# VectorE in place of GpSimd for the token groups' sums and lower halves, one per chunk, and a second buffer for w2's quarters

## The chip, the cores and the metric

The kernel runs on one core of a Trainium2 chip. Its time is the device time of one execution in microseconds (us); before the change the median of 3 runs is 772.16 us (771.65 to 772.54). Engines are named as in the profile: PE is TensorE, DVE is VectorE, ACT is ScalarE, POOL is GpSimd, SP issues the DMAs. Each engine's instructions stand in one order, that of the program.

## What is computed

Attention with sink tokens and a window, then a Fourier mix and a feed-forward layer over 4 x 768 tokens of 512 features:

```python
x = attention(q, k, v, n_sink, window)        # (4, 768, 512)
u = x + real(fft(fft(x, axis=1), axis=2))
un = (u - mean(u)) / sqrt(var(u) + 1e-6)      # over the features
out = u + maximum(un @ w_ch1, 0) @ w_ch2      # 512 -> 2048 -> 512
```

## The kernel before, in words

Attention and the Fourier mix of the four batches come first, up to about 265 us of the profile and at the end beside the first group; none of that is touched. The feed-forward layer then works through 24 blocks of 128 tokens in six groups of four blocks. All of its matmuls run on pairs: a float32 operand is split into an upper half, rounded to the type that PE takes (ACT's cast), and a lower half, which is the operand minus its upper half (a subtraction that reads two tiles in SBUF), and a product takes three matmuls (upper x upper, upper x lower, lower x upper).

**First group (231 to 336 us).** Plain products. Meanwhile the weights arrive, are split, and the seven combinations of w1 that the later groups need are stored to DRAM. At its end `prepare_1` makes the second group's tokens ready.

**Second group (group 1, 337 to 432 us).** The first layer uses seven products in place of eight for a 2 x 2 block matrix (Strassen and Winograd's scheme). `product(n, k, ps)` (L1350) is one of them: 12 matmuls of 256 columns, k = 0 to 6, for each of four chunks `it` of hidden features, into three PSUM banks A, B, C in the order `BANK = "ABCABCB"`; a bank is accumulated on again as soon as DVE or ACT has read it. DVE and ACT add the seven up into four quarters of the hidden layer; `halves` splits a quarter into a slot of `hring` (ACT L1151 upper with the relu, DVE L1152 lower), and `unit` (L1378, 12 matmuls of 512 columns) is the plain second layer of one quarter, one or two quarters behind.

Beside this, `step()` is called ten times for each chunk (40 in all) and plays two tables. `todo` prepares the third group's tokens: `statistics`, `deviate` (14 tiny DVE operations that make 1/sqrt), `make` (L543, the normalized block `un`, one buffer), `turn` (PE transposes it, ACT copies it to `xf`). `w2_at` makes the second layer's weight combinations for the later groups, for eight pairs p of weight tiles: `whole_w2` (DVE L1397, two operations: the whole w2 from its halves, into `sums_r`), `sums_w2` (POOL L1402 to L1405, four operations that read `sums_r`), `split_w2` (ACT L1409 and POOL L1410, twice each), `store_w2` (SP L1415, four DMAs to `td`). `sums_r` has one buffer, so DVE's `whole_w2` of the next pair waits until POOL has read this one. With the last chunk, `sums(2, G)` forms the third group's sums of token quarters (s2, s1, s4 at the chunk's start, s5 later) and their halves x: sums and lower halves on POOL (L1250 to L1261), upper halves on ACT (L1260).

**Last four groups (groups 2 to 5, 432 to 762 us).** Both layers use seven products. The first layer (L1350 again) runs 28 chunks of 12 matmuls; DVE and ACT make from them the quarters X1 to X4 and t, and POOL has its share: X3 = t - X1 and t = X4 + X3 (L1604, L1605) right behind k = 6, and X1 += t (`s1_h`, L1567). The second layer, `product2` (L1517), runs 28 chunks `s2` of 12 matmuls. For chunk s2 + 4, `upper_h` (ACT L1560) and `lower_h` (DVE L1564) split one hidden tile into `hring`, which has four slots: the upper half waits until PE is through with chunk s2. In the same 28 chunks POOL forms X2 -= t at k = 3 (L1635); DVE adds finished PSUM banks to u (`add_u`, L1523: three at once after k = 0), and `sums_x` makes the next group's seven token operands x: sums on POOL (L1542 to L1549), lower halves on DVE or POOL (L1539). Weights stream through eight places of `places`, a load being issued eight products ahead (`load`, L1324).

DVE and POOL both read and write SBUF; the four groups' PSUM reads are DVE's and ACT's.

Of the kernel before, what the change touches and what calls it, by code (L numbers as in the profile page):

```python
# [205 lines left out]
def kernel(  # L206
# [67 lines left out]
    def run(general):  # L274
        tag = "g" if general else ""
        with ExitStack() as p1:
# [942 lines left out]
            def prepare_1():  # L1219
                statistics, deviate, make, turn = prepare(1)  # L1220
                for i in range(4):
                    statistics(i)
                    yield
                for i, _ in enumerate(deviations(*groups[1][0], 4)):
                    if i % 4 == 3:
                        yield
                yield
                for i in range(4):
                    make(i)
                    yield  # L1230
                    turn(i, banks[1][0], "n")
                    yield
                start, put = sums(1, V)
                start()
                for k in range(7):
                    yield
                    put(k)

            def sums(n, eng):

                xf = state["xf"]
                a11, a12, a21, a22 = (xf[:, i, 2 * j:2 * j + 2] for i in range(2) for j in range(2))
                sm = state.setdefault("s", {})

                def new(k):
                    sm[k] = npool.tile([P, 2, 256], F32, tag="qs0", name=f"s{k}_{n}", bufs=QSB)
                    return sm[k]

                def start():
                    eng.tensor_tensor(new(2), a21, a22, op=ALU.add)  # L1250
                    eng.tensor_tensor(new(1), sm[2], a11, op=ALU.subtract)
                    eng.tensor_tensor(new(4), a11, a21, op=ALU.subtract)

                def put(k):
                    if k == 5:
                        eng.tensor_tensor(new(5), a12, sm[1], op=ALU.subtract)
                    x = {0: a11, 3: a12, 6: a22}.get(k)
                    x = sm[k] if x is None else x
                    hi, lo = (t[:, k].rearrange("p (c t) -> p c t", c=2) for t in state["x"])
                    A.copy(hi, x)  # L1260
                    eng.tensor_tensor(lo, x, f32(hi), op=ALU.subtract)  # L1261

                return start, put

# [68 lines left out]
            with tc.manual_schedule():  # L1333
# [60 lines left out]
                def whole_w2(p):  # L1394
                    for j in range(2):
                        w = Wt[2 * p + j, 1]
                        V.tensor_tensor(sums_r[:, j], f32(w[0]), f32(w[1]), op=ALU.add)  # L1397

                def sums_w2(p):
                    q = [sums_t[p % 2][i // 2][1][:, i % 2] for i in range(4)]  # L1400
                    b11, b12, b21, b22 = (sums_r[:, i, 256 * j:256 * j + 256] for i in range(2) for j in range(2))
                    G.tensor_tensor(q[1], b12, b11, op=ALU.subtract)  # L1402
                    G.tensor_tensor(q[0], b22, q[1], op=ALU.subtract)
                    G.tensor_tensor(q[2], b12, b22, op=ALU.subtract)
# [22 lines left out]
                for n in range(LDB, NWS):  # L1427
                    load(n)
                n = 0
                statistics, deviate, make, turn = prepare(2)  # L1430
                todo = {0: [(statistics, 0)], 1: [(statistics, 1, 2)], 2: [(statistics, 3)], 3: [(deviate,)], 4: [(make, 0)], 6: [(turn, 0, *banks[1][:2]), (make, 1)],
                        8: [(turn, 1, *banks[1][:2]), (make, 2)], 11: [(turn, 2, *banks[0][:2]), (make, 3)], 13: [(turn, 3, *banks[0][:2])]}
                turn_ = 0
                for it in range(NIT):
                    put = lambda k: None
                    if it == NIT - 1:
                        start, put = sums(2, G)
                        start()

                    def step():  # L1440
# [7 lines left out]
                    for k in range(7):  # L1448
# [33 lines left out]
                        step()  # L1482
                while done[0] < len(units):
                    unit(1)
                assert not w2_at, w2_at
# [17 lines left out]
                def get(i, b, name):  # L1503
                    pool, t = sets[i]["ABC".index(b)]
                    return pool.tile([P, 512], F32, tag=t, name=name, bufs=1)

                def product2(s2, k, c, n, ps):
                    h = hring[:, s2 % 4]
# [21 lines left out]
                def sums_x(g):  # L1530

                    xf = state["xf"]
                    a11, a12, a21, a22 = (xf[:, i, 2 * j:2 * j + 2] for i in range(2) for j in range(2))
                    s2 = npool.tile([P, 2, 256], F32, tag="un", name=f"sx_{g}", bufs=1)

                    def put(k, x, eng):
                        hi, lo = (t[:, k].rearrange("p (c t) -> p c t", c=2) for t in state["x"])
                        A.copy(hi, x)
                        eng.tensor_tensor(lo, x, f32(hi), op=ALU.subtract)  # L1539

                    return {
                        6: lambda: G.tensor_tensor(a21, a11, a21, op=ALU.subtract),  # L1542
                        7: lambda: G.tensor_tensor(s2, a22, a21, op=ALU.subtract),
                        8: lambda: put(0, a11, V),
                        9: lambda: put(3, a12, G),
                        10: lambda: put(1, s2, V),
                        11: lambda: G.tensor_tensor(a11, a11, s2, op=ALU.add),
                        14: lambda: put(4, a21, V),
                        16: lambda: G.tensor_tensor(a12, a12, s2, op=ALU.subtract),  # L1549
                        17: lambda: put(2, a11, G),  # L1550
                        19: lambda: put(5, a12, G),
                        21: lambda: put(6, a22, V),
                    }

                def upper_h(n):

# [7 lines left out]
                    V.tensor_tensor(*args, op=ALU.subtract)  # L1564

                def s1_h(c):
                    G.tensor_tensor(X[1][c], X[1][c], t_[c], op=ALU.add)  # L1567

                for g in range(2, len(groups)):
                    more_ = g + 1 < len(groups)  # L1570
                    todo = {}
# [6 lines left out]
                    for it in range(0, NIT, 2):  # L1578
                        for k in range(7):
                            for i in range(2):  # L1580
# [32 lines left out]
                                if t in (16, 17):  # L1613
                                    s1_h(t - 16)
                                for fn, *args in todo.pop(t - (7 if g > 2 else 0), ()):
                                    fn(*args)
                                t += 1
                    assert not todo
# [2 lines left out]
                    for s2 in range(7 * NIT):  # L1621
# [9 lines left out]
                            lower_h(s2 + 4, upper_h(s2 + 4))  # L1631
                        if s2 < 2:
                            s1_h(2 + s2)
                        if k == 3:
                            G.tensor_tensor(X[2][c], X[2][c], t_[c], op=ALU.subtract)  # L1635
                        if c == NIT - 1:
                            for half, m in (((0, 1), (1, 0), (1, 1)), ((0, 1),), ((1, 1),), ((0, 0),), ((1, 1),), ((0, 1),), ((1, 0),))[k]:
                                add_u(g, half, m, p)
                            if k >= 5:
                                store_u(g, k - 5)  # L1640
                        if g == 2 and 6 <= s2 < 6 + NPR:
                            f = s2 - 6
                            for a in range(2):
                                nc.sync.dma_start(f32(Wt[2 * f, 1][a])[:, 256:], t_dram[f][:, 3, 256 * a:256 * a + 256])
                        if s2 in xs:
                            xs[s2]()

    run(False)
    general = nc.values_load(outside[0:1, 0:1])
# [79 lines left out]
```

## Time and profile before

| what | before |
|---|---|
| median of 3 runs | 772.16 us |
| the profiled execution | 770.74 us |
| its span in the profile | 769.0 us |
| PE busy | 725.7 us (94%) |
| DVE busy | 555.6 us (72%) |
| POOL busy | 410.6 us (53%) |
| ACT busy | 350.0 us (46%) |
| chain that ended last | PE 63%, DVE 20%, POOL 7% |

The profiled execution took 1.74 us more than its span and 1.42 us less than the median. In the profile a line such as `493.64 1.77 DVE L1564 TENSOR_TENSOR hring<-x,hring` reads: start, duration, engine, line of the kernel, operation, the tile written and the tiles read, then shape and type and how many instructions were merged; in brackets the idle time of the engine ahead of it and who ended it. PEclk is the clock that PE was granted, as a share of the full one.

### The profile page before, as it was taken

Reading aid. Unit: us, or ns where it says so; the run is one execution under the profiler, and the core shown is the slowest. Engines: PE = TensorE matmul, PEld = TensorE weight load, DVE = VectorE, ACT = ScalarE, POOL = GpSimd, SP = SyncE. Lnnn points to the kernel's source line nnn. Section 1 sums busy time; section 2 is a strip of 40 time slices with the busy share of each in tenths; the row PEclk is TensorE's granted clock in tenths of the full one; section 3 lists DMA queues with packets and bytes.
Section 4 is the critical chain, followed back from the end, with each engine's and each line's share of the span. In section 5 each row is a group of like instructions: output and inputs, shape, how many; then the busy total and the mean of one; then the engine's idle time right before and its main releaser. Section 6 shows DMA issues by size and latency. Waiting matters only on the chain.

```text
span 769.0 us, 15770 instructions
## 1 busy us (share of the span) xinstructions
PE 725.7 (94%) x5539; PEld 646.3 (84%) x5539; DVE 555.6 (72%) x1251; ACT 350.0 (46%) x887; POOL 410.6 (53%) x487
## 2 busy tenths in 40 slices
PE   7999999989989889899989999999999999999996
PEld 5676876867878767678779999899998999899996
DVE  6877577887899988876763745957599467943683
ACT  4787666667533235413323244433454144523441
POOL 2567477476557878725978134810485046603430
PEclk9999999999999999999999999999999999999998
DMA  9863535432218798799988698959974897659731
GB/s 305 259 168 113 155 85 171 141 115 97 97 55 284 249 340 300 255 326 380 300 290 250 236 354 287 314 195 393 346 268 128 299 390 248 227 191 394 280 108 60
DMA packets 109577, 181.70 MB, mean 236 GB/s; under 512 B 9868, under 2 KB 44812, under 8 KB 108336
## 3 DMA queue, kind: packets, MB, share of 16 engines
q1 hardware_dynamic: 109200, 176.83, 67.7%
q0 software_dynamic: 288, 3.76, 1.2%
q8 instruction: 46, 0.75, 0.4%
q14 instruction: 43, 0.35, 0.1%
HBM read 148.04 MB, written 32.51 MB: 235 GB/s over the span
## 4 chain that ended last, share of the span: by engine, by line
PE 63%; DVE 20%; POOL 7%; issue 5%; ACT 3%; DMA 2%; SPq 0%; DVEq 0%; ACTq 0%; POOLq 0%
PE qB L1517 9%; PE pB L1350 9%; PE pA L1350 6%; PE qC L1517 6%; PE pC L1350 6%; PE qA L1517 4%; PE xt L839 4%; PE s L744 4%; PE o L1378 3%; PE pt L801 2%; PE za L398 2%; PE h L661 2%; DVE sm L763 1%; PE o L1159 1%; DVE hring L1564 1%
## 5 line engine op out<-in xcount | busy, mean ns | idle before, releaser
L1604 POOL TENSOR_TENSOR x<-u,x 128x512 f32<-128x512 f32 x16 | 22.8, 1427 | 163.0 <-ACT u L1603 163.0
L1564 DVE TENSOR_TENSOR hring<-x,hring 128x512 fp32r<-128x512 f32 x92 | 88.9, 993 | 6.2 <-ACT hring L1560 5.7
L1560 ACT CAST hring<-x 128x512 fp32r<-128x512 f32 x92 | 56.9, 618 | 54.9 <-PE qB L1517 15.8
L769 ACT ACTIVATE sm<-sm,mx 128x132 f32<-128x132 f32 x192 | 76.0, 400 | 4.9 <-DVE mx L763 4.9
L1350 PE MATMUL pB<-x,w_b 128*128 128x256 f32 x528 | 68.2, 283 | 0.0
L1350 PEld LDWEIGHTS pB<-x,w_b 128*128 128x128 f32 x528 | 64.9, 191 | 0.1
L661 PE MATMUL h<-un_slots,w_ring 128*128 128x512 f32 x192 | 50.4, 411 | 7.1 <-DVE h L1152 6.9
L744 PE MATMUL s<-ring,q 64*128 64x260 f32 x320 | 49.2, 411 | 7.5 <-DVE mx L763 3.7
L763 DVE CUSTOM_DVE_ANT_0 sm<-s,mask 128x132 f32<-128x132 f32 x192 | 48.5, 293 | 7.5 <-PE s L742 1.9
L661 PEld LDWEIGHTS h<-un_slots,w_ring 128*128 128x128 f32 x192 | 36.6, 197 | 17.1 <-DVE h L1152 6.7
L1350 PE MATMUL pC<-x,w_b 128*128 128x256 f32 x336 | 42.5, 281 | 2.6 <-DVE tmp L1471 2.6
L744 PEld LDWEIGHTS s<-ring,q 64*128 64x128 f32 x320 | 26.9, 185 | 20.1 <-issue 5.0
L1517 PE MATMUL qA<-w,hring 128*128 128x256 f32 x312 | 40.7, 281 | 3.1 <-DVE hring L1564 3.1
L1350 PEld LDWEIGHTS pC<-x,w_b 128*128 128x128 f32 x336 | 40.7, 189 | 3.4 <-DVE tmp L1471 3.3
L780 POOL CAST sk<-sm 128x32 fp32r<-128x32 f32 x48 | 11.1, 232 | 58.2 <-ACT sm L769 58.1
L1517 PEld LDWEIGHTS qA<-w,hring 128*128 128x128 f32 x312 | 38.2, 189 | 3.7 <-DVE hring L1564 3.7
L1159 PE MATMUL o<-w,h 128*128 128x512 f32 x156 | 39.1, 395 | 1.0 <-POOL w L629 0.4
L808 ACT COPY pta<-pt 128x512 f32<-128x512 f32 x48 | 28.1, 585 | 26.0 <-PE pt L801 25.9
L1378 PE MATMUL o<-w,hring 128*128 128x512 f32 x156 | 38.4, 393 | 1.4 <-DVE hring L1152 1.4
L839 PE MATMUL xt<-ptl,ldv 128*64 128x128 f32 x384 | 39.3, 285 | 0.0
L1517 PE MATMUL qB<-w_c,hring 128*128 128x256 f32 x288 | 37.6, 284 | 0.2
L817 POOL TENSOR_SCALAR_AFFINE_SELECT ptl<-pta 128x512 f32<-128x512 f32 x48 | 31.3, 652 | 11.6 <-ACT pta L808 11.6
(289 smaller groups left out, 1996.1 us busy)
## 6 DMA issues: line engine op xcount, KB each, us to landing
w_b<-wd SPq DMA_DIRECT2D x184, 256.0 KB, 4.8
w_c<-wd SPq DMA_DIRECT2D x96, 256.0 KB, 5.0
raw<-in_moe_w_ch_dram SPq DMA_DIRECT2D x32, 512.0 KB, 4.9
w_c<-td SPq DMA_DIRECT2D x48, 256.0 KB, 4.4
w_b<-td SPq DMA_DIRECT2D x48, 256.0 KB, 5.4
wd<-to SPq DMA_DIRECT2D x8, 1024.0 KB, 5.1
ldv<-in_v_dram SPq DMA_DIRECT2D x28, 256.0 KB, 3.0
ring<-in_qk_dram SPq DMA_DIRECT2D x24, 264.0 KB, 4.5
```

The costliest lines, as they stand in the source:

```text
L661: T.matmul(ps[:, :tb], a[cc], x[:, :, cc, :], start=n == 0, stop=n == 3 * NCC - 1)
L744: T.matmul(ps[:, j, :P + W], st["q", g][rows, hp, :], keys(g, 2 * hp + j), start=True, stop=True)
L763: V.tensor_tensor_reduce(sm[:, h % 4], ps[:, j, P:P + W], mask[min(qi, 3)], -SCALE, 3.0e38, ALU.add, ALU.min, accum_out=mx[:, 0, h:h + 1])
L769: A.activation(sm[:, h % 4], sm[:, h % 4], AF.Exp, bias=mx[:, 0, h:h + 1], scale=-1.0, accum_out=mx[:, 1, h:h + 1])
L817: G.affine_select(lo, a, [[0, 4], [s, P]], compare_op=ALU.is_ge, fill=0.0, base=0, channel_multiplier=-s)
L839: T.matmul(ps[D * j:D * j + D, p, :], st["v", kb(g) - i][:, h, :], a[:, h % 4, :], start=i == 0, stop=i == n - 1)
L1159: T.matmul(po[i], a[:, ts_], x, start=f == 0 and n == 0, stop=f == NF - 1 and n == 2)
L1350: T.matmul(ps[:, 256 * j:256 * j + 256], w[:, j, a, cs], x[:, xs], start=BANK.index(BANK[k]) == k and j == c == m == 0, stop=j == c == 1 a ...
L1378: T.matmul(po[i], h[:, a, j, ts_], x, start=first and j == m == 0, stop=last and j == 1 and m == 2)
L1517: T.matmul(ps[:, 256 * t:256 * t + 256], h[:, a, j, P * t:P * t + P], x, start=BANK.index(BANK[k]) == k and c == t == j == m == 0, stop=c ...
L1560: A.copy(hi, x)
L1564: V.tensor_tensor(*args, op=ALU.subtract)
```

## The change

Three edits, all in the feed-forward part:

1. **Last four groups.** X3, t, X1 += t, X2 -= t, the token sums and all their lower halves go from POOL to DVE; POOL gets no work there. They are placed by chunk so that a chunk has one of them: `sums_x` becomes a table of single operations, with s5 and the halves of x5 and x6 moved into the next group's first layer (`NSTEP + 1` to `NSTEP + 5`); `ADDS` spreads the three `add_u` of bank A over three chunks; X3 and t of the first two chunks wait for chunks 14 and 15, those of the last two stand together at the end of the first layer (t = 27).
2. **Second group, w2.** `sums_r` gets a second buffer, used by every other pair (a tile with the tag `qs0` for one half, `last_chunk` for the other). `whole_w2` comes one step later, `sums_w2` two later, `split_w2` and `store_w2` one later.
3. **Second group, tokens.** `sums` runs on DVE alone; the lower half of x(k) is issued with the upper half of x(k+1). `deviate` is cut in two, seven operations at step 3 and seven at step 5, with the first `make` and `turn` one step later.

The core of the diff:

```diff
-                def deviate():
-                    for _ in deviations(*first, len(us)):
-                        pass
+                dev = deviations(*first, len(us))
+                def deviate(n=None):
+                    while n != 0 and next(dev, 0) != 0:
+                        n = n and n - 1
...
-            def sums(n, eng):
+            def sums(n):
...
-                    eng.tensor_tensor(new(2), a21, a22, op=ALU.add)
-                    eng.tensor_tensor(new(1), sm[2], a11, op=ALU.subtract)
-                    eng.tensor_tensor(new(4), a11, a21, op=ALU.subtract)
+                    V.tensor_tensor(new(2), a21, a22, op=ALU.add)
+                    V.tensor_tensor(new(1), sm[2], a11, op=ALU.subtract)
+                    V.tensor_tensor(new(4), a11, a21, op=ALU.subtract)
...
-                    eng.tensor_tensor(lo, x, f32(hi), op=ALU.subtract)
+                        sm["lower"] = lo, x, f32(hi)
+                    if lower:
+                        V.tensor_tensor(*lower, op=ALU.subtract)
...
+                sums_r = [[sums_r[:, 0], sums_r[:, 1]], [npool.tile([P, 512], F32, tag="qs0", name="sums_r2", bufs=QSB), last_chunk]]
...
-                        V.tensor_tensor(sums_r[:, j], f32(w[0]), f32(w[1]), op=ALU.add)
+                        V.tensor_tensor(sums_r[p % 2][j], f32(w[0]), f32(w[1]), op=ALU.add)
...
-                    t0 = 4 + 25 * p // NPR
-                    for d, fn in ((0, whole_w2), (1, sums_w2), (4, split_w2), (5, store_w2)):
-                        w2_at.setdefault(t0 + d, []).append((fn, p))
+                    for t, fn in ((5 + 3 * p if p else 6, whole_w2), (7 + 3 * p, sums_w2), (9 + 3 * p, split_w2), (10 + 3 * p, store_w2)):
+                        w2_at.setdefault(t, []).append((fn, p))
...
-                todo = {0: [(statistics, 0)], 1: [(statistics, 1, 2)], 2: [(statistics, 3)], 3: [(deviate,)], 4: [(make, 0)], 6: [(turn, 0, *banks[1][:2]), (make, 1)],
+                todo = {0: [(statistics, 0)], 1: [(statistics, 1, 2)], 2: [(statistics, 3)], 3: [(deviate, 7)], 5: [(deviate,), (make, 0)], 7: [(turn, 0, *banks[1][:2]), (make, 1)],
...
-                        6: lambda: G.tensor_tensor(a21, a11, a21, op=ALU.subtract),
-                        7: lambda: G.tensor_tensor(s2, a22, a21, op=ALU.subtract),
-                        8: lambda: put(0, a11, V),
-                        9: lambda: put(3, a12, G),
...
+                        2: (s, a21, a11, a21, ALU.subtract),
+                        6: (s, s2, a22, a21, ALU.subtract),
+                        7: (hi, 0),
+                        8: (lo, 0),
...
+                        NSTEP + 1: (s, a12, a12, s2, ALU.subtract),
...
+                ADDS = {3: ("A", 0, 1), 4: ("A", 1, 0), 5: ("A", 1, 1), 7: ("B", 0, 1), 11: ("C", 1, 1), 15: ("A", 0, 0),
+                        19: ("B", 1, 1), 23: ("C", 0, 1), 27: ("B", 1, 0)}
...
-                    G.tensor_tensor(X[1][c], X[1][c], t_[c], op=ALU.add)
+                    V.tensor_tensor(X[1][c], X[1][c], t_[c], op=ALU.add)
...
-                                    G.tensor_tensor(X[3][c], t_[c], X[1][c], op=ALU.subtract)
-                                    G.tensor_tensor(t_[c], X[4][c], X[3][c], op=ALU.add)
+                                if t in (14, 15, 27):
+                                    for c_ in (2, 3) if t == 27 else (t - 14,):
+                                        V.tensor_tensor(X[3][c_], t_[c_], X[1][c_], op=ALU.subtract)
+                                        V.tensor_tensor(t_[c_], X[4][c_], X[3][c_], op=ALU.add)
...
-                        if k == 3:
-                            G.tensor_tensor(X[2][c], X[2][c], t_[c], op=ALU.subtract)
+                        if s2 in (9, 10, 12, 13):
+                            c_ = (9, 10, 12, 13).index(s2)
+                            V.tensor_tensor(X[2][c_], X[2][c_], t_[c_], op=ALU.subtract)
```

What moves on the engines shows at three places. The first is DVE in the second group's second chunk, before: `sums_r` is written by `whole_w2`, `un` by `make`, `hring` gets the lower half of the chunk's first quarter.

```order
L1397 TENSOR_TENSOR sums_r<-w_gh,w_gl 128x512 [waits Pool_49] x2
L1460 TENSOR_TENSOR tmp<-pB_1_4576,tmp 128x512 [waits PE_49,Activation_49]
L543 TENSOR_SCALAR un_5_4610<-u_65,stat_2_4364 128x512 [waits PE_49]
L1397 TENSOR_TENSOR sums_r<-w_gh,w_gl 128x512 [waits DVE_49,Pool_49]
L1397 TENSOR_TENSOR sums_r<-w_0_3711,w_1_3712 128x512 [waits DVE_49,Pool_49]
L1152 SCALAR_TENSOR_TENSOR hring<-pA_1_4558,hring 128x512 [waits Activation_49]
```

The same place in the changed program (`sums_r_4335` and `last_chunk` are the second buffer):

```order
L1469 TENSOR_TENSOR tmp<-pB_1_4575,tmp 128x512 [waits PE_49,Activation_49]
L543 TENSOR_SCALAR un_5_4609<-u_65,stat_2_4365 128x512 [waits PE_49]
L1407 TENSOR_TENSOR sums_r<-w_gh,w_gl 128x512 [waits Pool_49] x2
L1152 SCALAR_TENSOR_TENSOR hring<-pA_1_4551,hring 128x512 [waits Activation_49]
L1407 TENSOR_TENSOR sums_r_4335<-w_gh,w_gl 128x512 [waits Pool_49]
L1407 TENSOR_TENSOR last_chunk<-w_0_3711,w_1_3712 128x512 [waits Pool_49]
```

The lower half into `hring` now stands ahead of the fourth pair's `whole_w2`, and that one writes another buffer than the pair before it. The second place is the start of the last chunk (it = 3) of the second group. There POOL had, before, the sums `s`, two of which wait for a DMA's semaphore, and then the lower halves of x:

```order
L1250 TENSOR_TENSOR s_2_4986<-xf 128x512
L1251 TENSOR_TENSOR s_2_4988<-s_2_4986,xf 128x512 [waits DMAHW7_49,Pool_49]
L1252 TENSOR_TENSOR s_2_4990<-xf 128x512 [waits DMAHW1_49]
L1261 TENSOR_TENSOR x_3702<-xf,x_3701 128x512 [waits Activation_49]
L1261 TENSOR_TENSOR x_3702<-s_2_4988,x_3701 128x512 [waits Activation_49]
```

DVE in the changed program at that place:

```order
L1152 SCALAR_TENSOR_TENSOR hring<-tmp,hring 128x512 [waits Activation_49]
L1255 TENSOR_TENSOR s_2_4983<-xf 128x512 [waits Pool_49]
L1256 TENSOR_TENSOR s_2_4985<-s_2_4983,xf 128x512 [waits DMAHW1_49,DVE_49,Pool_49]
L1257 TENSOR_TENSOR s_2_4987<-xf 128x512 [waits DMAHW3_49,Pool_49]
L1270 TENSOR_TENSOR x_3702<-xf,x_3701 128x512 [waits Activation_49]
L1469 TENSOR_TENSOR tmp<-pB_3_5010,tmp 128x512 [waits PE_49,Activation_49]
L1270 TENSOR_TENSOR x_3702<-s_2_4985,x_3701 128x512 [waits Activation_49]
L1270 TENSOR_TENSOR x_3702<-s_2_4983,x_3701 128x512 [waits Activation_49]
L1152 SCALAR_TENSOR_TENSOR hring<-pA_3_4989,hring 128x512 [waits PE_49,Activation_49]
```

The two waits for a DMA stand on DVE now, ahead of its read of bank B (L1469) and of the quarter's lower half (L1152). The DMAs are the stores of the eighth pair's `sums_q`, whose places in SBUF the new sums take; on SP these stores stand one load pair later than before. The third place is DVE in a second layer, chunks 11 to 15. Before:

```order
L1523 TENSOR_TENSOR u_65<-qC_5869,u_65 128x2x256
L1564 TENSOR_TENSOR hring<-x_0_5208,hring 128x512 [waits PE_49,Activation_49] x2
L1564 TENSOR_TENSOR hring<-x_1_5209,hring 128x512 [waits PE_49,Activation_49]
L1539 TENSOR_TENSOR x_3702<-xf,x_3701 128x512 [waits Activation_49]
L1564 TENSOR_TENSOR hring<-x_1_5209,hring 128x512 [waits PE_49,Activation_49]
```

Now:

```order
L1535 TENSOR_TENSOR u_65<-qC_5871,u_65 128x2x256
L1595 TENSOR_TENSOR hring<-x_0_5209,hring 128x512 [waits PE_49,Activation_49]
L1673 TENSOR_TENSOR x_5208<-x_5208,u_65 128x512 [waits DVE_49]
L1595 TENSOR_TENSOR hring<-x_0_5209,hring 128x512 [waits PE_49,Activation_49]
L1673 TENSOR_TENSOR x_5208<-x_5208,u_65 128x512 [waits DVE_49]
L1595 TENSOR_TENSOR hring<-x_1_5210,hring 128x512 [waits PE_49,Activation_49]
L1556 TENSOR_TENSOR x_3702<-sx_5735,x_3701 128x512
L1595 TENSOR_TENSOR hring<-x_1_5210,hring 128x512 [waits PE_49,Activation_49]
```

Each lower half into `hring` has one other operation behind it, which was POOL's (X2, L1673) or DVE's in another chunk.

More of the change, by code (lines that the diff above doesn't have):

```diff
@@ L1232, in prepare_1 @@
                     yield
-                start, put = sums(1, V)
+                start, put = sums(1)
                 start()
@@ L1237, in prepare_1 @@
                     put(k)
-            def sums(n, eng):
+                    if k < 6:
+                        continue
+                    put(7)
+            def sums(n):
                 xf = state["xf"]
@@ L1249, in start @@
                 def start():
-                    eng.tensor_tensor(new(2), a21, a22, op=ALU.add)
-                    eng.tensor_tensor(new(1), sm[2], a11, op=ALU.subtract)
-                    eng.tensor_tensor(new(4), a11, a21, op=ALU.subtract)
+                    V.tensor_tensor(new(2), a21, a22, op=ALU.add)
+                    V.tensor_tensor(new(1), sm[2], a11, op=ALU.subtract)
+                    V.tensor_tensor(new(4), a11, a21, op=ALU.subtract)
                 def put(k):
[L1255 to L1260, printed above, removed]
-                    eng.tensor_tensor(lo, x, f32(hi), op=ALU.subtract)
+                    lower = sm.pop("lower", None)
+                    if k < 7:
+                        if k == 5:
+                            V.tensor_tensor(new(5), a12, sm[1], op=ALU.subtract)
+                        x = {0: a11, 3: a12, 6: a22}.get(k)
+                        x = sm[k] if x is None else x
+                        hi, lo = (t[:, k].rearrange("p (c t) -> p c t", c=2) for t in state["x"])
+                        A.copy(hi, x)
+                        sm["lower"] = lo, x, f32(hi)
+                    if lower:
+                        V.tensor_tensor(*lower, op=ALU.subtract)
                 return start, put
@@ L1396, in whole_w2 @@
                         w = Wt[2 * p + j, 1]
-                        V.tensor_tensor(sums_r[:, j], f32(w[0]), f32(w[1]), op=ALU.add)
+                        V.tensor_tensor(sums_r[p % 2][j], f32(w[0]), f32(w[1]), op=ALU.add)
                 def sums_w2(p):
                     q = [sums_t[p % 2][i // 2][1][:, i % 2] for i in range(4)]
-                    b11, b12, b21, b22 = (sums_r[:, i, 256 * j:256 * j + 256] for i in range(2) for j in range(2))
+                    b11, b12, b21, b22 = (sums_r[p % 2][i][:, 256 * j:256 * j + 256] for i in range(2) for j in range(2))
                     G.tensor_tensor(q[1], b12, b11, op=ALU.subtract)
@@ L1436, in run @@
                     if it == NIT - 1:
-                        start, put = sums(2, G)
+                        start, put = sums(2)
                         start()
@@ L1482, in run @@
                         step()
+                put(7)
                 while done[0] < len(units):
@@ L1534, in sums_x @@
                     s2 = npool.tile([P, 2, 256], F32, tag="un", name=f"sx_{g}", bufs=1)
[L1536 to L1539, printed above, removed]
-                    return {
-                        6: lambda: G.tensor_tensor(a21, a11, a21, op=ALU.subtract),
-                        7: lambda: G.tensor_tensor(s2, a22, a21, op=ALU.subtract),
-                        8: lambda: put(0, a11, V),
-                        9: lambda: put(3, a12, G),
[L1546 to L1552, printed above, removed]
-                    }
+                    form = (a11, s2, a11, a12, a21, a12, a22)
@@ new lines, in halves, with hi, lo, s @@
+                    def halves(k):
+                        return [t[:, k].rearrange("p (c t) -> p c t", c=2) for t in state["x"]]
+                    def hi(k):
+                        A.copy(halves(k)[0], form[k])
+                    def lo(k):
+                        V.tensor_tensor(halves(k)[1], form[k], f32(halves(k)[0]), op=ALU.subtract)
+                    def s(o, a, b, op):
+                        V.tensor_tensor(o, a, b, op=op)
+                    return {
+                        2: (s, a21, a11, a21, ALU.subtract),
+                        6: (s, s2, a22, a21, ALU.subtract),
+                        7: (hi, 0),
+                        8: (lo, 0),
+                        13: (hi, 1),
+                        14: (lo, 1),
+                        15: (hi, 3),
+                        16: (lo, 3),
+                        17: (s, a11, a11, s2, ALU.add),
+                        18: (hi, 4),
+                        19: (lo, 4),
+                        20: (hi, 2),
+                        21: (lo, 2),
+                        NSTEP + 1: (s, a12, a12, s2, ALU.subtract),
+                        NSTEP + 2: (hi, 6),
+                        NSTEP + 3: (lo, 6),
+                        NSTEP + 4: (hi, 5),
+                        NSTEP + 5: (lo, 5),
+                    }
@@ L1633, in run @@
                             s1_h(2 + s2)
-                        if k == 3:
[L1635 to L1640, printed above, removed]
+                        if s2 in (9, 10, 12, 13):
+                            c_ = (9, 10, 12, 13).index(s2)
+                            V.tensor_tensor(X[2][c_], X[2][c_], t_[c_], op=ALU.subtract)
+                        if s2 in ADDS:
+                            b, half, m = ADDS[s2]
+                            add_u(g, half, m, ps[b])
+                            if s2 in (23, 27):
+                                store_u(g, half)
                         if g == 2 and 6 <= s2 < 6 + NPR:
@@ L1645, in run @@
                         if s2 in xs:
-                            xs[s2]()
+                            fn, *args = xs[s2]
+                            fn(*args)
     run(False)
```

5 lines of the change are left out of this document (added).

## Prediction

> **What bounds the kernel now.** I read the page first, then PE's waits behind 336 us, then the windows of the four second layers, then timelines where PE waits.
>
> ```profile
> span 769.0 us, 15770 instructions
> PE 725.7 (94%) x5539; PEld 646.3 (84%) x5539; DVE 555.6 (72%) x1251; ACT 350.0 (46%) x887; POOL 410.6 (53%) x487
> ```
>
> PE is the bound: the change adds and removes no matmul, so it can only give back time in which PE stands still.
>
> ```profile
> engine line waited for: us in total, times, longest us
> PE o L1378 <- DVE hring L1152: 3.1, 2, 1.7
> PE qA L1517 <- DVE hring L1564: 3.1, 3, 1.1
> PE pC L1350 <- DVE tmp L1471: 2.6, 1, 2.6
> PE unt L549 <- DVE un L543: 1.7, 3, 0.7
> ```
>
> In the touched part (336 to 769 us) PE waits for DVE alone, in few places. Waits are counted net, without the slow matmuls behind them; the second layers show the whole loss. The four windows run from a layer's first qA to its last matmul:
>
> ```profile
> core 0: us, PE busy (x) PEld busy (x) DVE busy (x) ACT busy (x) POOL busy (x), PEclk, DMA share, GB/s
> 472.51:514.73 42.22, 41.14 (x338) 40.05 (x338) 35.72 (x37) 19.22 (x33) 26.97 (x17) 1.00 0.75 253
> 556.61:598.83 42.22, 41.09 (x338) 40.04 (x338) 35.99 (x37) 19.18 (x32) 27.03 (x17) 1.00 0.59 199
> 640.83:683.04 42.21, 41.11 (x338) 40.07 (x338) 35.95 (x37) 19.19 (x32) 26.99 (x17) 1.00 0.58 200
> 722.39:762.03 39.64, 39.62 (x337) 39.42 (x335) 27.52 (x33) 15.57 (x26) 15.35 (x10) 1.00 0.31 107
> ```
>
> The fourth does the same matmuls but prepares no next group; it takes 39.64 us, 1.416 us for each of its 28 chunks. The other three lose 2.58, 2.58 and 2.57 us. How, the timeline of the first shows, and that of the last what DVE does when POOL leaves it alone:
>
> ```profile
> 487.34 0.68 DVE L1564 TENSOR_TENSOR hring<-x,hring 128x512 fp32r<-128x512 f32 x1
> 491.44 6.82 POOL L1635 TENSOR_TENSOR x<-x,u 128x512 f32<-128x512 f32 x4
> 493.64 1.77 DVE L1564 TENSOR_TENSOR hring<-x,hring 128x512 fp32r<-128x512 f32 x1
> 495.47 1.45 PE L1517 MATMUL qA<-w,hring 128*128 128x256 f32 x10 [1.03 <-DVE hring L1564]
> ...
> 745.66 0.69 DVE L1564 TENSOR_TENSOR hring<-x,hring 128x512 fp32r<-128x512 f32 x1 [0.67 <-ACT hring L1560]
> 746.27 0.68 DVE L1523 TENSOR_TENSOR u<-qA,u 128x512 f32<-128x512 f32 x1
> ```
>
> The same subtraction takes 0.68 us, but 1.77 us beside a run of POOL's, and the late lower half is what PE waits for. Two DVE operations that don't need each other start 0.61 us apart.
>
> **Part 1, the second layers of groups 2 to 4.** All of POOL's work there goes, and with it what stretches DVE. DVE now has in a second layer 24 lower halves for `hring`, 4 X2, 2 X1, 9 `add_u`, 5 lower halves of x and 3 token sums: 47 operations, at 0.61 to 0.69 us 28.7 to 32.4 us of 39.64. By chunk it is the lower half plus one, 1.22 to 1.38 us of 1.416; chunk 19 has two more, and chunks 18 and 20 one less. Lower halves are issued four chunks ahead and their slot comes free one chunk later, so DVE may be some 2.8 us late before PE waits. I take the fourth window as what the other three become: 7.7 us, less 0.1 for remnants, **-7.6 us**. Bounds: 0, if DVE stays stretched, and 7.7.
>
> In the first layers DVE gains 13 operations a group, 9 us at most. A 40 us window in the first layer of the fifth group:
>
> ```profile
> 600.00:640.00 40.00, 39.28 (x338) 39.08 (x337) 23.09 (x49) 14.99 (x26) 7.88 (x6) 1.00 1.00 362
> ```
>
> DVE uses 23.09 there, so it has room. Of PE's three waits for `un` two (1.0 of 1.7 us) lie in first layers, behind `deviate`, which is not moved there: no change. The four moved operations at t = 27 follow PE's last matmul: a bank read, X3, t, X3, t and the next lower half, with two dependent pairs, end at about 4.0 us; PE needs that lower half after four chunks, at 5.7 us. Covered by 1.6 us. The last layer has no tokens to prepare: no change, nor in the tail (1.74 us outside the span).
>
> **Part 2, the second group.** PE's and DVE's rows at its stalls:
>
> ```profile
> 345.41 0.17 DVE L535 SCALAR_TENSOR_TENSOR stat<-stat 128x4 f32<-128x4 f32 x1
> 345.49 0.69 DVE L1152 SCALAR_TENSOR_TENSOR hring<-pA,hring 128x512 fp32r<-128x512 f32 x1
> 346.23 2.57 PE L1378 MATMUL o<-w,hring 128*128 128x512 f32 x10 [1.42 <-DVE hring L1152]
> ...
> 350.47 0.95 DVE L543 TENSOR_SCALAR un<-u,stat 128x512 f32<-128x512 f32 x1
> 351.57 0.63 PE L549 MATMUL unt<-ident,un 128*128 128x128 f32 x4 [0.68 <-DVE un L543]
> ...
> 368.45 1.21 DVE L1397 TENSOR_TENSOR sums_r<-w_gh,w_gl 128x512 f32<-128x512 f32 x1 [5.32 <-POOL tmp L1404]
> 371.27 0.68 DVE L1152 SCALAR_TENSOR_TENSOR hring<-pA,hring 128x512 fp32r<-128x512 f32 x1
> 372.01 0.73 PE L1378 MATMUL o<-w_gh,hring 128*128 128x512 f32 x2 [1.73 <-DVE hring L1152]
> ...
> 394.90 1.81 DVE L1397 TENSOR_TENSOR sums_r<-w,w 128x512 f32<-128x512 f32 x2 [2.78 <-POOL tmp L1404]
> 397.34 0.69 DVE L1471 TENSOR_TENSOR tmp<-tmp,pC 128x512 f32<-128x512 f32 x1
> 398.08 2.05 PE L1350 MATMUL pC<-x,w_b 128*128 128x256 f32 x12 [2.61 <-DVE tmp L1471]
> ```
>
> (a) `deviate` in two parts puts L1152 seven tiny operations earlier: 1.3 us less at the first stall. But the second `un` now stands behind them and both `whole_w2` operations; on DVE it ends near 351.2 us, hardly before the old 351.42. PE arrives earlier and waits longer there: **-0.4** (0 to -1.3).
>
> (b) At 368 us DVE waits 5.32 us for POOL to be done with the one buffer, and L1152 stands behind. With two buffers, and L1152 ahead, the wait goes: **-1.9** (1.73 and the slow matmul behind it).
>
> (c) The same at 394.90: **-2.8**. This stall also cost clock:
>
> ```profile
> 395.77:399.18 3.41, 1.10 (x9) 1.10 (x10) 2.68 (x5) 1.12 (x3) 0.00 (x0) 1.00 0.35 118
> 399.18:402.59 3.41, 3.41 (x18) 3.41 (x18) 1.79 (x3) 1.18 (x3) 3.25 (x3) 0.50 0.54 191
> ```
>
> After 3.41 us in which PE was busy for 1.10, it got half the clock for 3.41 us: **-1.7** when the stall goes.
>
> (d) What comes in its place: the token sums. Two of them now wait on DVE for the store of the last pair's `sums_q`, and bank B's read (L1469), which PE needs for k = 4, is queued behind. POOL's pace decides when that store leaves, and the rows of the stores give their latency:
>
> ```profile
> 366.16:392.62 26.46, 25.51 (x25) 1.00 1.01 327
> ...
> 408.81 0.79 SPq L1415 DMA_DIRECT2D td<-sums_q  x1
> 411.75 1.30 POOL L1251 TENSOR_TENSOR s<-s,xf 128x512 f32<-128x512 f32 x1 [2.21 <-DMA td<-sums_q]
> 413.54 1.30 POOL L1252 TENSOR_TENSOR s<-xf 128x512 f32<-128x512 f32 x1 [0.49 <-DMA td<-sums_q]
> ...
> 405.31 1.52 PE L1350 MATMUL pA<-x,w_b 128*128 128x256 f32 x12
> 406.67 1.52 PE L1350 MATMUL pB<-x,w_b 128*128 128x256 f32 x12
> 408.03 2.91 PE L1378 MATMUL o<-w,hring 128*128 128x512 f32 x12
> 410.78 1.52 PE L1350 MATMUL pC<-x,w_b 128*128 128x256 f32 x12
> ```
>
> The first row is POOL's alone, four pairs in 26.46 us, 6.6 us each and no idle time; the store lands at most 3.9 us after its issue (409.60 to 413.54). A product takes 1.36 us of PE, a `unit` 2.75 (from start to start). I put the start of the second pair's sums on POOL near 360 us in the new order (ACT's copies for the first pair now wait behind the chunk's last quarter). Then pair 8 starts at 360 + 6 x 6.6 = 399.6, its `split_w2` ends at 406.2, the store is issued some 0.4 later and lands at 410.5, and DVE is through L1257, one lower half and L1469 at 412.2. PE, without (a) to (c), starts the last chunk at 405.3 - 6.8 = 398.5 and reaches k = 4 after four products and two `unit`s, 4 x 1.36 + 2 x 2.75 = 10.9 us, at 409.4. So it waits **+2.8** us. Bounds: 0, if POOL, less often held up by DVE, gains those 2.8 us by then; 6.1, if it comes half a pair later. ACT stands in the same queue (it copies those sums, then makes the relu), but DVE's lower half is later than both.
>
> On the clock, the row above has 2.3 us of idle PE in a window of 3.41 before the halving, so a stall of 2.8 can trigger it as well, if it falls into one window: +1.7, with about four chances in ten; not in the sum. By the Trainium skill ("TensorE: Matmul & The Clock Gate", Part 1) the clock is halved after at least one idle window of about 3.4 us; by that rule no stall of 2.8 us would cost clock, and this trace differs from it.
>
> SP's queue: the stores stand one load pair later, and the loads behind them can wait for POOL; with eight places ahead, over 11 us, PE should not notice. The first group and its `prepare_1` keep their order.
>
> Sum for the second group: -0.4 - 1.9 - 2.8 - 1.7 + 2.8 = **-4.0** (+1.4 to -7.7, the upper end with 1.7 of clock).
>
> **Rivals.**
> - *Slower: DVE becomes the bound of the second layers.* If the stretched 1.77 us isn't POOL's doing but DVE's own price for reading two tiles in SBUF in this stage, all moved operations pay it. The point is 39.64 / 47 = 0.84 us per operation. At 1.15 us for the 38 that read two tiles there and 0.61 for nine `add_u`, a layer takes 49.2 us, 7.0 over now, three times: 770.7 + 21 - 4.0 + 1.4 = 789. Against it: 0.68 us at 487.34 and 0.69 at 745.66. The Trainium skill ("Perfetto Trace Analysis", Optimizing Scalar/DVE Operations) advises moving work from a saturated DVE to GpSimd, and doubts it in the same breath for the port that they share; here 82% of a layer is DVE's upper estimate, so I don't count it saturated.
> - *The second group gains nothing:* the new wait (d) is at its upper bound, 6.1 us, and halves the clock: -4.0 + 3.3 + 1.7 = +1.0, in all 770.7 - 7.6 + 1.0 + 1.4 = 765.5. For it: POOL has no idle time in that row, and DVE's remaining two-tile reads still collide with it.
> - *The burst at t = 27 is late* by 1.4 us more than its cover, once in each of four groups: +5.6, 760.5 + 5.6 = 766. Against it: ACT and PE have no other work for DVE there.
>
> **How the numbers follow.** Against the profiled execution: 770.74 - 7.6 - 4.0 = 759.1. That execution lies 1.42 us under the median of 772.16, and I forecast for medians: **760.5 us**. Chances: forecast 0.66, second group without gain 0.18, late burst 0.08, DVE as the bound 0.08. The likeliest case alone reaches from 757 (no new wait) to 762 (new wait with clock); with the second and third case the range is 757 to 766. A measurement tells apart about 0.2%, 1.5 us: faster 0.90, the same 0.02 (rivals two and three together), slower 0.08.
>
> **What would show it.** Right: second layers of 39.6 to 40.0 us with no DVE lower half above 0.7 us and POOL idle behind the second group; no PE wait at 369 and 395 us and full clock near 400; one PE wait of 1 to 4 us in the second group's last chunk, ended by DVE's L1469 behind sums that wait for a store. Wrong: lower halves that stay over 1 us, PE waits spread over the second layers, or a second group that still takes 95 us.

## The result and the profile after

The changed kernel takes 767.23 us (median of 11 runs, 764.31 to 770.43), the one before 772.54 us in the same comparison. The ratio is 0.9921, with a 95% interval of 0.9900 to 0.9942: faster by 0.8%, where 1.5% was forecast. 767.23 us also lies above the range of the forecast. The page of the profile after:

```profile
span 765.6 us, 15721 instructions
PE 723.0 (94%) x5539; PEld 647.0 (85%) x5539; DVE 569.5 (74%) x1347; ACT 350.5 (46%) x887; POOL 270.0 (35%) x391
```

The four second layers, from first qA to last matmul, in the view of windows:

```profile
core 0: us, PE busy (x) PEld busy (x) DVE busy (x) ACT busy (x) POOL busy (x), PEclk, DMA share, GB/s
476.09:515.71 39.62, 39.62 (x339) 39.62 (x337) 32.40 (x51) 18.31 (x31) 0.00 (x0) 1.00 0.81 275
557.37:596.99 39.62, 39.62 (x339) 39.62 (x337) 32.39 (x51) 18.25 (x31) 0.00 (x0) 1.00 0.62 210
639.83:679.44 39.61, 39.61 (x338) 39.61 (x337) 32.41 (x51) 18.25 (x31) 0.00 (x0) 1.00 0.62 211
718.79:758.41 39.62, 39.62 (x338) 39.58 (x336) 27.95 (x43) 15.71 (x26) 0.00 (x0) 1.00 0.33 114
```

All four now take what the last one took: 42.22, 42.22 and 42.21 us became 39.62, 39.62 and 39.61. PE is busy in all of that time; DVE, with 32.4 us of work, holds it up nowhere. Part 1 gave 7.8 us. DVE now does 51 operations of a layer in 32.40 us, where 37 took 35.72 beside POOL. This part of the change both empties POOL and spreads DVE's operations over the chunks; what each of the two is worth by itself was not tried. The waits behind 336 us (engine, what it works on, whom it waited for: total, times, longest) show what was lost:

```profile
engine line waited for: us in total, times, longest us
DVE s L1256 <- DMA td<-sums_q: 7.6, 1, 7.6
PE pB L1359 <- DVE tmp L1469: 5.0, 1, 5.0
PE unt L549 <- DVE un L543: 2.8, 3, 1.3
```

The waits of PE for L1152 at 369 us and for L1471 at 395 us are gone; one wait of 5.0 us has come. Its place in the timeline, DVE first, then PE; then PE alone by windows of 3.41 us (length, PE busy and its matmuls, granted clock, DMA share, GB/s):

```profile
414.17 0.69 DVE L1256 TENSOR_TENSOR s<-s,xf 128x512 f32<-128x512 f32 x1 [7.61 <-DMA td<-sums_q]
415.22 0.69 DVE L1257 TENSOR_TENSOR s<-xf 128x512 f32<-128x512 f32 x1 [0.35 <-DMA td<-sums_q]
...
416.43 0.69 DVE L1469 TENSOR_TENSOR tmp<-pB,tmp 128x512 f32<-128x512 f32 x1
```

```profile
409.25 2.91 PE L1387 MATMUL o<-w,hring 128*128 128x512 f32 x12
417.17 2.93 PE L1359 MATMUL pB<-x,w_c 128*128 128x256 f32 x12 [5.00 <-DVE tmp L1469]
419.89 4.51 PE L1387 MATMUL o<-w,hring 128*128 128x512 f32 x12
```

```profile
413.07:416.48 3.41, 0.00 (x0) 1.00 0.80 303
416.48:419.89 3.41, 2.72 (x12) 0.50 0.07 10
419.89:423.31 3.42, 3.42 (x10) 0.50 0.48 149
423.31:426.72 3.41, 3.41 (x27) 1.00 0.16 21
```

DVE's second sum waits 7.61 us for the store of the last pair's `sums_q`. L1469, the read of bank B, ends at 417.12 us, and PE's fifth product of the chunk starts right behind it. Then PE runs at half the clock for two windows: the 12 products of 512 columns at 419.89 take 4.35 us from start to start, where 2.75 is usual.

A table of the second group, from its first product to the third group's first product, and what it loses against matmuls at their usual distance (118 and 229 ns):

| the second group, us | before | after |
|---|---|---|
| its length | 94.95 | 96.57 |
| lost in the first chunk (336 to 354 us) | 3.3 | 3.3 |
| lost at 369 us | 2.0 | 0 |
| lost at 395 us, and to the clock behind it | 2.8 + 1.5 | 0 |
| lost at 412 us, and to the clock behind it | 0 | 5.2 + 2.9 |

It became 1.6 us longer, where 4.0 us less was forecast. The two profiled executions differ at one more place: after reaches its second group 2.1 us later (338.68 against 336.56 us). The first experiment has before's code up to there and reaches it at 338.32 us, and two kernels with the changed code reach it at 337.40 and 336.71 us, so that these 2.1 us are no effect of the change. Without them the stages give -7.8 + 1.6 + 0.6 (the first layers) = -5.6 us, and the medians differ by 5.3. The 0.6 us are no effect of the change either, as far as single executions tell: with the same code in the last four groups, the kernel of the third run below takes 163.9 us for its four first layers, before 164.1.

### The profile page after: what moved, and what is told of

The parts are those of the page before. It is cut to its first block, busy times and chain, and to the rows that moved or that the text cites. A ratio compares the mean times of both kernels' runs of the same rounds, so it can differ in the third digit from the quotient of the medians.

```text
span 765.6 us, 15721 instructions
## 1 busy us (share of the span) xinstructions
PE 723.0 (94%) x5539; PEld 647.0 (85%) x5539; DVE 569.5 (74%) x1347; ACT 350.5 (46%) x887; POOL 270.0 (35%) x391
## 4 chain that ended last, share of the span: by engine, by line
PE 66%; DVE 16%; POOL 7%; issue 4%; DMA 3%; ACT 3%; SPq 1%; DVEq 0%; ACTq 0%; POOLq 0%
PE pB L1359 9%; PE qB L1529 9%; PE pA L1359 6%; PE qC L1529 6%; PE qA L1529 6%; PE pC L1359 5%; PE o L1387 4%; PE xt L839 4%; PE s L744 4%; PE pt L801 2%; PE h L661 2%; PE za L398 2%; PE o L1159 1%; PE zb L398 1%; DVE sm L763 1%
## 5 line engine op out<-in xcount | busy, mean ns | idle before, releaser
L1595 DVE TENSOR_TENSOR hring<-x,hring 128x512 fp32r<-128x512 f32 x92 | 63.5, 690 | 15.0 <-ACT hring L1591 9.3
L1159 PEld LDWEIGHTS o<-w,h 128*128 128x128 f32 x156 | 29.3, 190 | 9.1 <-ACT h L1151 1.4
L769 ACT ACTIVATION_READ_ACCUMULATOR sm<-sm,mx 128x1 f32 x192 | 36.8, 191 | 0.0
L1529 PE MATMUL qB<-w_c,hring 128*128 128x256 f32 x288 | 35.2, 281 | 0.0
```

What stands on the lines that cost most here:

```text
L769: A.activation(sm[:, h % 4], sm[:, h % 4], AF.Exp, bias=mx[:, 0, h:h + 1], scale=-1.0, accum_out=mx[:, 1, h:h + 1])
L1159: T.matmul(po[i], a[:, ts_], x, start=f == 0 and n == 0, stop=f == NF - 1 and n == 2)
L1529: T.matmul(ps[:, 256 * t:256 * t + 256], h[:, a, j, P * t:P * t + P], x, start=BANK.index(BANK[k]) == k and c == t == j == m == 0, stop=c ...
```

## The experiments

Theory S says that the missing 6 us lie in the second group: the new stall behind the store, and the clock behind it. Its rival G says that the second layers' gain is given back elsewhere, and that the second group is neutral.

**One part alone, and the other.** The first kernel has before's code up to the second group's end and the changed code behind it, the second the reverse:

```diff
 # first: the kernel before up to "assert not w2_at", the changed kernel behind it
 # second: the changed kernel up to there, the kernel before behind it
```

> Only the edits of the last four groups; the second group is as before. Theory S (the missing 6 us lie in the second group: a stall of 5.2 us behind the store and 2.9 us of halved clock): the second layers take 39.6 us, nothing else moves, 772.5 - 7.8 = 764.7 us, ratio 0.990. Rival G (the second layers' gain is given back elsewhere in the program, in first layers or ahead of 336 us, and the second group is neutral): about 767 us, ratio 0.993, as with the whole change.

> Only the second group's edits; the last four groups are as before. Theory S: the stalls at 369 and 395 us go (4.8 us, and 1.6 of clock), the stall behind the store comes (5.2 and 2.9): 772.5 + 1.9 = 774.4 us, ratio 1.0025. Rival G: no change or a gain, ratio 1.000 or below.

The first took 764.53 us, ratio 0.9896 (0.9877 to 0.9915): second layers of 39.6 us and a second group of 94.14 us. The second took 774.86 us, ratio 1.0022 (1.0005 to 1.0040): second layers of 42.2 to 42.3 us and a second group of 96.29 us. Two of PE's waits in the second group of the second kernel:

```profile
PE pB L1359 <- DVE tmp L1469: 5.4, 1, 5.4
PE pB L1359 <- DMA w_b<-wd: 1.0, 1, 1.0
```

Both came out as S has it. The second group's edits, taken alone, make the kernel slower by 0.2%, and the first part alone beats the whole change. G falls.

**The same wait, one pair earlier.** The set of places that a pair's combinations use is swapped, so that the last pair is stored from `tmp` and `sums_q` is free a pair earlier:

```diff
-                sums_t = [sums_t, [(sums_h[:, i]..., sums_q[i]) for i in range(2)]]
+                sums_t = [[(sums_h[:, i]..., sums_q[i]) for i in range(2)], sums_t]
```

> The change with the two sets of places for w2's combinations swapped: the last pair is stored from tmp, the last but one from sums_q, so that the sums wait for a store one pair (6.7 us) earlier. Theory S: no PE wait of over 0.5 us at the last chunk's bank B and full clock there; 767.2 - 8.1 = 759 us, ratio 0.983. Rival G: the wait moves to another place or costs nothing; 766 us or more, ratio 0.992.

It took 757.44 us, ratio 0.9819 (0.9794 to 0.9843). The second group takes 88.66 us, 7.9 less than in the changed kernel. DVE and PE in its last chunk:

```profile
404.59 1.67 DVE L1256 TENSOR_TENSOR s<-s,xf 128x512 f32<-128x512 f32 x1
406.18 1.79 DVE L1257 TENSOR_TENSOR s<-xf 128x512 f32<-128x512 f32 x1
...
408.49 0.68 DVE L1469 TENSOR_TENSOR tmp<-pB,tmp 128x512 f32<-128x512 f32 x1
```

```profile
410.08 1.61 PE L1359 MATMUL pB<-x,w_c 128*128 128x256 f32 x12
```

Neither of these sums waits for a store, L1469 ends at 409.17 us, and PE comes for the bank at 410.08 without a wait. One swapped line gives back the whole stall and the clock, though these two sums run beside POOL there and take 1.67 and 1.79 us, where they took 0.69 each in the changed kernel, with POOL done.

**The sums behind the bank's read.** They wait for the same store, but L1469 is ahead of them:

```diff
                         elif k == 1:
                             V.tensor_tensor(u2, b, p1c, op=ALU.add)
+                            if it == NIT - 1:
+                                start()
+                                put(1)
```

> The change with the three token sums issued behind DVE's read of bank B (k = 1) in place of ahead of it; they wait for the same store. Theory S: what costs is the read queued behind the wait, so PE's wait at k = 4 goes; DVE comes free at 416 us, and PE reaches the next product that needs it near 417, so at most 1 us of a new wait: 760 us, ratio 0.984. Rival G: 766 us or more. If PE then waits at k = 6 for 3 us or more with the clock halved again, ratio 0.990, DVE's wait itself is what counts, wherever it stands.

It took 767.54 us, ratio 0.9919 (0.9894 to 0.9944): nothing gained. In its profiled execution (770.15 us) the last chunk loses 6.3 us in place of 8.0, and the stall for `un` in the first chunk costs 1.6 us of clock there. S was wrong on where the next wait would be, right that DVE is held (8.15 us here). PE, then ACT:

```profile
421.60 0.73 PE L1387 MATMUL o<-w,hring 128*128 128x512 f32 x2 [3.89 <-ACT hring L1151]
422.82 3.91 PE L1387 MATMUL o<-w,hring 128*128 128x512 f32 x10 [0.48 <-DVE hring L1152]
```

```profile
419.40 1.14 ACT L1267 CAST x<-s 128x512 fp32r<-128x512 f32 x2 [8.82 <-DVE s L1256]
...
420.96 0.59 ACT L1151 ACTIVATE hring<-pA 128x512 fp32r<-128x512 f32 x1
```

The product on bank B is no longer late, but the `unit` behind it needs the quarter of k = 3, whose two halves are queued behind the held sums: on ACT behind the copies of x, on DVE behind the sums. Two engines stood in the queue, and so the wait moves by one step of PE. I had counted only the product at k = 6.

**What else the edits are worth.** Three more kernels: two orders on DVE, `deviate` in one piece again, and the sums on POOL. The kernel before took 773.82 us beside these three, and 772.89 us beside the four above, so the ratios are what compares:

```diff
 # first, on the kernel with the swap
-  (5 + 3 * p if p else 6, whole_w2)   ...   todo.pop(t - (7 if g > 2 else 0), ())
+  (5 + 3 * p if p else 7, whole_w2)   ...   todo.pop(t - (8 if g > 2 else 0), ())
 # second, on the kernel with the swap
-  3: [(deviate, 7)], 5: [(deviate,), (make, 0)], 7: [(turn, 0, ...), (make, 1)],
+  3: [(deviate,)], 4: [(make, 0)], 6: [(turn, 0, ...), (make, 1)],
 # third, on the changed kernel: sums(2) on G, and every step of w2_at one earlier
```

> The swap of places as in the third run, and two orders on DVE: in the second group's first chunk the second un stands ahead of the first pair's whole_w2, and in the last four groups each token step comes one product later. Theory S: what is left of PE's waits outside the first 336 us is for un (1.9 us at 350 us, up to 1.4 us in the first layers); they shrink to under 0.7 us each, 757.4 - 1.2 - 0.8 = 755.4 us, ratio 0.979. Rival: PE waits for the next thing there (a load, bank B's read) and the time stays at 757.4 us, ratio 0.982.

> The swap of places, with deviate in one piece and make and turn where they were before the change. Theory S: cutting deviate in two bought nothing, because loads and un hold PE in the same chunk: the waits of the second group's first chunk stay at 3 us together and the time at 757.4 us within 1 us. Rival: the cut is worth the 1.3 us of its first stall; 758.7 us and 4.3 us of waits in that chunk.

> The change with the second group's token sums and lower halves on GpSimd again, as before the change, and every w2 step one step earlier (so that the last pair's split stands ahead of the sums); the two buffers for w2 stay, and the sums take the places of the last pair's sums_q. Theory S: the stall comes from DVE being held by the store; GpSimd may wait for it without holding PE: no wait of over 0.7 us in the last chunk, 758 us, ratio 0.982. Rival: ACT, whose copies of the sums stand ahead of its relu, holds PE as DVE did, 2 us or more with halved clock: 762 us or more, ratio 0.987.

The first took 759.21 us, ratio 0.9828 (0.9795 to 0.9861), no gain over the swap alone. The `un` of the second group's first chunk did come earlier (that chunk loses 1.7 us in place of 3.3), but a token step moved by one product puts the 14 operations of `deviate` behind one more bank read, and in this profile the first layers of the fourth and fifth groups wait longer, 42.7 us in place of 41.9. That the order does it is not shown: with the order unmoved these layers take 41.6 to 42.9 us in the profiles here. One such wait:

```profile
611.45 0.66 PE L549 MATMUL unt<-ident,un 128*128 128x128 f32 x4 [1.63 <-DVE un L543]
```

The second took 757.14 us, ratio 0.9787 (0.9761 to 0.9813), with a second group of 87.67 us: cutting `deviate` in two bought nothing, and by the profile it costs 1.0 us (88.66). S had that chunk's waits stay at 3 us; without the cut it loses 2.3. PE's waits of the kernel with the cut, and of the one without:

```profile
PE unt L549 <- DVE un L543: 2.4, 3, 1.9
PE pB L1359 <- DVE stat L531: 0.7, 1, 0.7
```

```profile
PE pB L1359 <- DVE stat L533: 0.8, 1, 0.8
PE unt L549 <- DVE un L543: 0.5, 2, 0.3
PE o L1387 <- DVE hring L1152: 0.3, 1, 0.3
```

The second halves of `deviate` and both `whole_w2` stood ahead of the second `un`, as the prediction had it, and PE pays for that what it saves at L1152. (The wait put down to `stat` has nothing to do with `stat`: bank B had been read before, and with the second group's edits alone, above, the same product is put down to the load of `w_b`.) Its ratio is the lowest of all kernels here, but its interval overlaps that of the swap with the cut.

The third, with the sums on POOL, took 762.18 us, ratio 0.9852 (0.9824 to 0.9881). PE waits for nothing in its last chunk, so ACT doesn't hold it there as the rival had it; but ACT's casts for a pair, one step earlier, now wait for POOL with a relu behind them (this one 0.77 us, the one ahead of it 4.34), DVE's lower half waits for that relu with `whole_w2` and a bank read behind it, and PE loses 2.0 us between 391 and 397 us:

```profile
391.13 0.62 ACT L1419 CAST sums_h<-sums_q 128x512 fp32r<-128x512 f32 x1 [0.77 <-POOL sums_q L1415]
391.65 0.59 ACT L1151 ACTIVATE hring<-pA 128x512 fp32r<-128x512 f32 x1
```

This kernel doesn't tell what it was meant to: the store lands early enough in it (POOL's second sum starts at 409.85 us, and PE comes for bank B only at 413.60) that DVE might have waited for it too.

**The price of a stall in clock.** In the kernel with the swap the read of bank B is repeated on DVE; the copies write the same sum again:

```diff
-                            V.tensor_tensor(u2, b, p1c, op=ALU.add)
+                            for _ in range(1 if it < NIT - 1 else 1 + 4):   # 6, 10
+                                V.tensor_tensor(u2, b, p1c, op=ALU.add)
```

> The kernel with the swapped places (no stall in the last chunk), with DVE's read of bank B in the last chunk issued 4 times more; the copies write the same sum again. PE has 0.9 us of slack there, so 4 x 0.6 to 0.7 us make a stall of 1.5 to 2.0 us. Theory S (a stall of PE itself brings the halved clock): like the 2.0 us stall of the first chunk there, this one is followed by full clock, price 1.7 us. Rival L (the halved clock after the change's stall came from the loads and stores that crowd there, not from the stall): the same, full clock.

> As before with 6 repeats: a stall of 2.8 to 3.3 us, as long as the one of before at 395 us. Theory S: half clock for about 3.4 us behind it, price 3 + 1.6 us. Rival L: full clock, price 3 us.

> As before with 10 repeats: a stall of 5.2 to 6.0 us, as long as the change's own. Theory S: half clock for 5 to 7 us, price 5.5 + 2.9 us. Rival L: full clock, price 5.5 us.

One run each, 763.33, 763.61 and 766.16 us, beside 775.40 of before; the stalls were 2.0, 3.2 and 6.3 us. PE by the clock's own windows, for 4, 6 (two places) and 10 repeats:

```profile
411.94:415.35 3.41, 1.74 (x8) 1.00 1.08 374
415.35:418.76 3.41, 3.13 (x19) 1.00 0.91 322
```

```profile
349.98:353.39 3.41, 1.54 (x13) 1.00 1.05 405
353.39:356.80 3.41, 3.41 (x17) 0.50 1.06 423
...
411.42:414.83 3.41, 1.98 (x9) 1.00 1.08 375
414.83:418.24 3.41, 1.62 (x13) 1.00 0.64 246
418.24:421.65 3.41, 3.41 (x20) 1.00 0.49 154
```

```profile
410.78:414.19 3.41, 0.70 (x4) 1.00 1.07 378
414.19:417.60 3.41, 0.00 (x0) 0.50 0.33 125
417.60:421.02 3.42, 3.29 (x14) 0.50 0.16 29
```

With 10 repeats the clock is halved for two windows as in the changed kernel, and no store or load was touched: the stall does it, and L falls. Its price is some 1.6 us, not the 2.9 that S gave, since PE stands still in the first of the two halved windows. But S was wrong for 6: a stall of 3.2 us costs no clock, because it lies across two windows and leaves PE busy for 1.98 and 1.62 us of them, while in the same run the stall for `un`, 2.0 us and whole in one window, halves it. What counts is PE's work in a window of a fixed grid, not the stall's length.

## Why the prediction was wrong

- **Part 1 was right.** -7.6 us forecast, -7.8 measured: no lower half over 0.70 us, no wait. DVE as the bound (789 us) and the late burst at t = 27 did not come.
- **(b) and (c) were right.** The two waits are gone, in this kernel and in the swap: 2.0, and 2.8 with 1.5 of clock; forecast 1.9, 2.8 and 1.7. In the swapped kernel, where nothing takes their place, the second group is 6.3 us shorter than before.
- **(a) was too high:** -0.4 forecast, 0 measured. The stall at L1152 went, and PE waits in its place at the product at 346.08 us (for a load, as argued above) and longer for `un`: the first chunk takes 19.57 us up to the next chunk's first product, before 19.64. In the kernel with the swap the group is 1.0 us shorter with `deviate` whole than with the cut.
- **(d) failed: "So it waits +2.8 us".** The wait was seen, with its cause and its place, but the term was sized at about half: it came to 5.2 us, within the bounds given (0 to 6.1). POOL's start was right: 360 us, measured 362.15 less the 2.1 that this run is late, 360.05. What was short: the last split ends at 408.97, 0.7 us later than worked out. The store then takes longer: DVE's two sums, released at 414.17 and 415.22 us, start 6.1 and 5.9 us after the stores were issued, where before's row gave 3.9:

```profile
407.74 0.37 SPq L1425 DMA_DIRECT2D td<-sums_q  x1
...
409.00 0.36 SPq L1425 DMA_DIRECT2D td<-sums_q  x1
```

The prediction took that latency from before, where the stores stand elsewhere among the loads. In the three kernels whose sums are on POOL (before, the first experiment, the third of the three kernels above) it is 3.6 to 4.9 us; in the three whose sums wait on DVE, 5.9 to 6.6. In the kernel with the swap nothing waits for the last pair's stores, and they still land 6.7 us after their issue (median of four), so the engine that waits is not the reason. What is stays open: the DMA engines' share between 409 and 413 us doesn't tell them apart (1.08 here, 1.09 before), and no run moves the loads alone.
- **The clock was left out of the sum.** "+1.7, with about four chances in ten; not in the sum": with the stall at 5.2 us the halving was no matter of chance. Wherever it starts, at least 2.6 us of it fall into one window of 3.41 us, more than the 2.3 us of the prediction's own row. It cost 2.9 us, two halved windows. The Trainium skill ("TensorE: Matmul & The Clock Gate", Part 1) has the halving follow an idle window of about 3.4 us, and says that these windows run on their own; the grid agrees with these runs. "Idle" does not: windows with PE busy for 1.54 or 1.55 us were followed by half the clock.
- The second rival, no gain in the second group at 765.5 us, comes nearest to what happened: it had -4.0 + 3.3 + 1.7 for (d) at 6.1 us, and measured is +1.6 with (d) at 5.2 and 2.9 of clock. It had a chance of 0.18. The prediction named for it that POOL has no idle time (its row has 25.51 us busy of 26.46); but POOL's pace held to 0.7 us, and the store's 2 us were the larger part of what (d) lacked.

In sum: (a) 0.4, (d) 2.4 and the clock 2.9 make the 5.7 us by which the second group was misjudged (1.6 + 4.0 = 5.6). The measured median lies 6.7 us above the forecast; the rest is the 0.6 us of the first layers and the kernel before, which was 0.4 us slower in this comparison than in the one that the forecast started from.

## What to carry to other kernels

Before an operation goes from a side engine to one that feeds PE, list what it waits for, a buffer's reuse too, and what stands behind it: what cost the side engine nothing can hold PE. Where a temporary reuses the place of a transfer's source, take that of an older transfer; here the swap of two sets of buffers was worth 8 us, more than the whole change. The move behind the bank's read shows that the order on one engine isn't enough: ACT stood in the same queue. And a stall is to be priced with its clock: from about 2 us on it can bring a halved window, and one that is full of work cost some 1.5 us more here.

## What the runs showed of the hardware

The granted clock changes on a grid of 3.41 us. Of the windows of full clock behind 336 us, those ahead of a halved one had PE busy for 1.55 us or less, and those with 1.60 us or more were followed by full clock, in all twelve profiles. Ahead of 336 us the border is less sharp: two windows with 1.65 and 1.71 us were followed by half the clock, and one with 1.51 us by full clock. It takes more to leave the halved state: behind 336 us a halved window with PE busy for 2.72 us, in the changed kernel, was followed by another, and the least that was followed by full clock is 2.93 us (in the kernel with the sums behind the read). A halved window full of work costs some 1.5 us of PE's time. So, by estimate from these bounds and for the stretch behind 336 us, a stall under 1.8 us by itself is not charged, one over some 3.7 us always is (1.86 us idle in a window, and twice that), and between them its phase decides: the wait at 395 us cost clock in before's profile, and the same wait in that of the first experiment didn't:

```profile
399.85 1.68 PE L1350 MATMUL pC<-x,w_b 128*128 128x256 f32 x12 [2.61 <-DVE tmp L1471]
```
